# A kernel of linear attention and two expert layers: transposing q as loaded, wider weight blocks, and a new order of the front

## The chip, the cores and the metric

One core of a Trainium2 chip runs the whole program. The metric is the device time of one execution in microseconds, from runs of the same program on the chip; the profile is of one execution of it. TensorE (PE) makes all matrix products and transposes, VectorE (DVE) and ScalarE (ACT) copy, add, split and square, GpSimd (POOL) clears tiles and takes the inverse roots, and SyncE (SP) issues nearly all transfers.

## What is computed

```python
kv = np.einsum('bhsd,bhse->bhde', k, v)          # 4 batches, 8 heads, 576 tokens, 64 wide
out = np.einsum('bhsd,bhde->bhse', q, kv)
out = out / np.sqrt(np.mean(out * out, -1) + 1e-06) * g_norm
x = out as [2304, 512]                            # heads side by side
x = ((x @ w1) * (x @ w2) @ w3) @ w_out            # float64 weights, d_ff 1024
p = domain_probs / domain_probs.sum(-1)           # 4 experts
out = sum over e of p[:, e] * (max(x @ e_w1[e], 0) @ e_w2[e])
```

## The kernel before

Every large product is split: an operand is kept as a high and a low part of a rounded 32-bit type (fp32r), and a product is three matmuls (`mm3`, L327 to L329), high by high, high by low and low by high. Many products are joined in a scheme of seven block products in place of eight, which needs sums of blocks of the weights (s1 to s4) and of the tokens (t1 to t4). The attention's own products are plain float32.

The order of the work on every engine is made ahead by a planner (`Plan`). Each step is added with the engines that could run it and a cost on each, what it reads and writes, and its delay (`latency`); `order` then runs through the steps with these costs and writes down one fixed sequence for each engine. The steps come in stages: the text `FRONT` lists those up to the experts, and the stage's number is the priority. Costs and delays are only the planner's; on the chip an engine waits for what its next instruction needs.

The front of the kernel. `constants` makes an identity and ten warm-up transposes of it (L424). A `unit b p` is one batch and two heads: it loads q, k and v as [128 partitions, 2 heads x 4 tokens x 64], which is 512 tokens with four to a partition; the remaining 64 tokens of all heads come through `rest_kv` as one tile of 64 partitions for each of k and v and a batch, with cleared partitions below (L571). Then

- `outer` (L717) makes kv of the two heads, each from 4 rounds of 128 tokens and one of the rest; head 0 goes to partitions 0 to 63 and columns 0 to 63 of a bank, head 1 to partitions 64 to 127 and columns 64 to 127. Two copies bring them to the diagonal blocks of `kvb`, a cleared tile for a batch (L670).
- `qs` is a copy of q with its columns in the order token, head (L733 on ScalarE, L734 on VectorE), so that a transpose (L688) gives both heads of one token round in one block; `inner` (L745) multiplies four such blocks by the diagonal block of `kvb`.
- `normed_turned` sums the squares (L596: eight ScalarE instructions with a running sum each), takes the inverse root on POOL (L608, L609), scales (L612), transposes (L688), multiplies by g and splits.

`rest_unit` does the inner products of the 64 remaining tokens of two batches (L780). g comes in as a column, one element for each partition (`load_norm`, issued by ScalarE). In stages 1, 2 and 3 the planner's loop puts 3, 3 and 2 transposes of the identity (L1822, "fillers") before a step that opens a new bank.

`weight n f` loads and decodes 128 columns and all 512 rows of w1 or w2 (float64, 512 KB). `bilinear_plain` and `bilinear_pair` multiply x by two of these each and multiply the results. After `mixed` and `mixed_product`, the experts run over three groups of 768 tokens: `up` makes the hidden layer of one pair of F blocks, `down` or `down_product` multiplies by the second layer. In the first group the expert's weights are loaded (`expert_weights`, two transfers for each layer and pair of blocks, i and i + 4), summed, split and stored to DRAM (`keep_w2`, L1317, one buffer for an expert); later steps load them back (`right_operand`, as `w`).

Of the kernel before, what the change touches and what calls it, by code (L numbers as in the profile page):

```python
# [31 lines left out]
SUMMING = 18  # L32
# [67 lines left out]
class Plan:  # L100
# [11 lines left out]
    def add(self, engines, emit, reads=(), writes=(), latency=0.2, stage=None, free=False, hold=None):  # L112
# [4 lines left out]

        op = Op(engines, emit, self.stage if stage is None else stage, latency)
# [24 lines left out]
    def order(self):  # L143
# [43 lines left out]
        while len(result) < len(ops):  # L187
# [9 lines left out]
            for e in engines:  # L197
# [26 lines left out]
                end = now + op.engines[e]  # L224
# [5 lines left out]
                op.done = end + op.latency  # L230
# [32 lines left out]
def attention_moe_kernel(  # L263
# [48 lines left out]
    plan = Plan({"r": RAWS, "h": TILES, "n": 4, "c": 2, "b": BANKS, "d": 1000, **RINGS})  # L312
# [33 lines left out]
    def load(buf, *parts, key=None, queue="sp", cost=None):  # L346
        def emit(_):
            for dst, src in parts:
                (nc.sync if queue == "sp" else nc.scalar).dma_start(
                    out=dst(buf.tile), in_=src[:, :] if isinstance(src, Buf) else src  # L350
                )

        add(
            {queue: cost or (1.48 if buf.kind == "r" else 0.68)}, emit,
            reads=[src for _, src in parts if isinstance(src, Buf)], writes=[(buf, key)], latency=2.6,
        )
# [54 lines left out]
    graw = const.tile([P, 1], F32, name="graw")  # L411
# [5 lines left out]
    def constants():  # L417
# [3 lines left out]
        nc.scalar.activation(out=graw, in_=ident[:, 0:1], func=ACTF.Square)  # L421
# [4 lines left out]
    def load_norm(_):  # L426
        for i in range(2):
            nc.scalar.dma_start(out=graw[i * D:(i + 1) * D], in_=g_norm.rearrange("(d o) -> d o", o=1))
        nc.vector.tensor_scalar(out=g8, in0=graw, scalar1=float(D) ** 0.5, scalar2=None, op0=ALU.mult)
# [19 lines left out]
    def decode(name, src, shape=None):  # L449
# [6 lines left out]
        load(raw, ((lambda t: t.rearrange("p (k f) -> p k f", k=KD)) if shape else whole, src))  # L456
# [110 lines left out]
    def rest_kv(b):  # L567

        kvr[b] = [half("kvr") for _ in (k, v)]
        for raw, src in zip(kvr[b], (k, v)):  # L570
            add({"pool": 0.4}, lambda _, raw=raw: nc.gpsimd.memset(raw[REM:P], 0.0), writes=[(raw, 1)])  # L571
            load(
                raw, (lambda t: t[0:REM].rearrange("p (h d) -> p h d", d=D), rest(src, b)),
                key=0, cost=1.05,
            )
# [3 lines left out]
    def normed_turned(ps, places, whole_values=None):  # L579
# [7 lines left out]
        summing = SUMMING > len(summed)  # L587
# [23 lines left out]
        def scale(e):  # L611
            nc.vector.tensor_tensor(  # L612
# [5 lines left out]
        if summing:  # L618
            add({"act": 8 * t_act(D, True)}, square, reads=[ps], writes=[t, ss])
# [3 lines left out]
        add({"pool": 1.91}, root, writes=[ss], hold=0.3)  # L623
# [44 lines left out]
    def zeroed(name):  # L668
        t = half(name)
        add({"pool": 0.5}, lambda _: nc.gpsimd.memset(t.tile, 0.0), writes=[t])  # L670
        return t
# [21 lines left out]
    def unit(b, p):  # L693
        first = b not in kvb
        if first:
            kvb[b] = zeroed("kvb")
        loaded = []
        for name, src in (("q", q), ("kv", k), ("kv", v)):
            raw = half(name, ring="attention")
            load(raw, (heads, head_pair(src, b, p)), cost=0.82)  # L700
            loaded.append(raw)
        qraw, ks, vs = loaded
        if first:
            rest_kv(b)
        kr, vr = kvr[b]
        ps = bank()

        def outer(e):
            for r in range(R + 1):
                for h in range(2):  # L710
                    c = slice(h * D, (h + 1) * D)
                    if r < R:
                        a, b_ = heads(ks.tile)[:, h, r, :], heads(vs.tile)[:, h, r, :]
                    else:
                        m = slice(p * P + h * D, p * P + (h + 1) * D)
                        a, b_ = kr[:, m], vr[:, m]
                    nc.tensor.matmul(ps[c, c], a, b_, start=r == 0, stop=r == R)  # L717

        add({"pe": 0.9}, outer, reads=[ks, vs, kr, vr], writes=[ps])
        for i in range(2):  # L720
            c = slice(i * D, (i + 1) * D)
            evacuate(
                kvb[b], ps, D, lambda t, i=i, c=c: t[c, p * P + i * D:p * P + (i + 1) * D],
                lambda t, c=c: t[c, c], key=(p, i),
            )
        qs = half("qs")

        def by_token(t):
            return t.rearrange("p (r h d) -> p h r d", r=R, h=2)

        add(
            {"act": t_act(512), "dve": t_fast(512)},
            lambda e: nc.scalar.copy(by_token(qs.tile), heads(qraw.tile)) if e == "act"  # L733
            else nc.vector.tensor_copy(out=by_token(qs.tile), in_=heads(qraw.tile)),  # L734
            reads=[qraw], writes=[qs],
        )
        pq = turned(qs)
# [9 lines left out]
        add({"pe": 0.86}, inner, reads=[qt, (kvb[b], (p, 0)), (kvb[b], (p, 1))], writes=[po])  # L747
        xr[b, p] = half("xr")
        if b == B - 1 and p < HP // 2:
            normed_turned(po, [], xr[b, p])  # L750
        else:
            xt[b, p] = Pair("xt")
            normed_turned(po, [(512, xt[b, p], whole, whole, None)], xr[b, p])

    def rest_unit(g):
# [4 lines left out]
            (lambda t: t[REM:P].rearrange("p (h d) -> p h d", d=D), rest(q, 2 * g + 1)), cost=1.5,  # L760
# [21 lines left out]
        add({"pe": 1.72}, inner, reads=[qs[0], qs[1], kvb[2 * g], kvb[2 * g + 1]], writes=[po])  # L782
# [16 lines left out]
    def first_product(w, xs, b):  # L799
# [3 lines left out]
        for k0 in range(0, KD, 2):  # L803
# [4 lines left out]
            def mms(_, k0=k0):  # L808
# [1046 lines left out]
```

## Time and profile before

| | us |
|---|---|
| median of 3 runs (1107.46 to 1109.48) | 1107.79 |
| the profiled execution | 1109.42 |
| its span, first to last instruction | 1107.6 |
| TensorE busy in the span | 1093.7 |
| VectorE / ScalarE / GpSimd busy | 864.2 / 616.5 / 47.0 |
| granted TensorE clock | full (2.4 GHz) in all slices |

Busy time is the union of an engine's instructions; matmuls are pipelined and their ends are modelled, so instructions that follow each other overlap, and the chain of waits, which lays them end to end, shows better what one of them costs.

### The profile page before, as it was taken

The numbers are of one execution on the slowest core, as the hardware profiler recorded it, in microseconds if no ns is written. First come the engines' busy times: TensorE is split into PE (matmuls) and PEld (weight loads), VectorE is DVE, ScalarE is ACT, GpSimd is POOL, SyncE is SP. The second block draws the span as 40 slices with busy tenths as digits, with TensorE's granted clock in tenths as the row PEclk, the third lists the DMA queues.
The fourth block names the chain that finished last, engine by engine and source line by source line (L and its number), as shares of the span: only waits on it lengthen the run. The fifth ranks groups of instructions, "written<-read, shape, count | busy, mean of one in ns | idle before, by whom it ended". The sixth has DMA issues, their size and how long they took to land.

```text
span 1107.6 us, 18599 instructions
## 1 busy us (share of the span) xinstructions
PE 1093.7 (99%) x6376; PEld 993.9 (90%) x6376; DVE 864.2 (78%) x1723; ACT 616.5 (56%) x1500; POOL 47.0 (4%) x57
## 2 busy tenths in 40 slices
PE   7999999999999999999999999999999999999998
PEld 6888888888888999999998999999999999999998
DVE  4888888889869887878888884557788866485896
ACT  6998754656636665754564465443455555444531
POOL 4513200000000000000000000000000000000000
PEclk9999999999999999999999999999999999999999
DMA  9999993441230499988999996878779877686856
GB/s 262 292 345 331 379 359 124 135 155 37 88 103 17 156 334 352 355 304 285 353 356 355 369 348 222 284 237 283 239 240 356 298 222 257 226 290 219 278 154 196
DMA packets 176862, 282.30 MB, mean 255 GB/s; under 512 B 22144, under 2 KB 89728, under 8 KB 176768
## 3 DMA queue, kind: packets, MB, share of 16 engines
q1 hardware_dynamic: 176448, 280.85, 76.1%
q8 instruction: 50, 0.82, 0.3%
q10 hardware_dynamic: 320, 0.26, 0.1%
q14 instruction: 44, 0.36, 0.1%
HBM read 198.22 MB, written 82.84 MB: 254 GB/s over the span
## 4 chain that ended last, share of the span: by engine, by line
PE 94%; DMA 3%; ACT 1%; POOL 1%; DVE 0%; issue 0%; SPq 0%; POOLq 0%; DVEq 0%
PE b L327 24%; PE b L329 24%; PE b L328 24%; PE b L1574 18%; PE b L688 2%; DMA kv<-in_v_dram 1%; PE b L745 1%; PE b L717 1%; DMA w<-w2kept 1%; DMA graw<-in_g_norm_dram 0%; POOL ss L609 0%; DMA we<-wel 0%; DMA woraw<-in_moe_w_out_dram 0%; PE b L780 0%; ACT x L596 0%
## 5 line engine op out<-in xcount | busy, mean ns | idle before, releaser
L676 ACT COPY u<-b 128x384 f32<-128x384 f32 (+1 forms) x191 | 96.4, 505 | 209.3 <-PE b L329 202.3
L1574 PE MATMUL b<-w,hth 128*128 128x512 f32 x588 | 208.2, 394 | 0.3 <-DVE acc L1602 0.2
L1410 DVE TENSOR_TENSOR u<-u,b 128x384 f32<-128x384 f32 x144 | 79.5, 552 | 117.9 <-PE b L329 59.3
L1574 PE MATMUL b<-w,htl 128*128 128x256 f32 x588 | 153.9, 279 | 0.0
L1574 PEld LDWEIGHTS b<-w,hth 128*128 128x128 f32 x588 | 108.4, 188 | 19.0 <-DVE acc L1602 0.9
L1574 PEld LDWEIGHTS b<-w,htl 128*128 128x128 f32 x588 | 110.6, 188 | 3.8
L1602 DVE SCALAR_TENSOR_TENSOR acc<-b,pn,acc 128x512 f32<-128x512 f32 x123 | 85.5, 745 | 29.1 <-PE b L1574 28.4
L372 ACT CAST hth<-s 128x384 fp32r<-128x384 f32 x144 | 70.0, 512 | 48.3 <-DVE s L1510 45.6
L1421 ACT ACTIVATE u<-u 128x384 f32<-128x384 f32 x108 | 56.9, 527 | 44.0 <-DVE u L1410 43.7
L377 DVE TENSOR_TENSOR htl<-s,hth 128x384 fp32r<-128x384 f32 x144 | 75.4, 551 | 3.4 <-ACT hth L372 3.1
L329 PE MATMUL b<-wdh,htl 128*128 128x512 f32 x144 | 56.7, 394 | 0.0
L377 DVE TENSOR_TENSOR htl<-u,hth 128x384 fp32r<-128x384 f32 x108 | 56.0, 551 | 0.8 <-ACT hth L372 0.7
L328 PE MATMUL b<-wdl,hth 128*128 128x512 f32 x144 | 56.6, 393 | 0.0
L327 PE MATMUL b<-wdh,hth 128*128 128x512 f32 x144 | 56.0, 389 | 0.0
L372 ACT CAST hth<-u 128x384 fp32r<-128x384 f32 x107 | 51.5, 510 | 2.4 <-PE b L329 2.0
L327 PE MATMUL b<-w,hth 128*128 128x256 f32 x168 | 47.6, 284 | 1.3 <-DMA w<-w2kept 1.3
L328 PE MATMUL b<-w,hth 128*128 128x256 f32 x168 | 47.5, 283 | 0.0
L329 PE MATMUL b<-w,htl 128*128 128x256 f32 x168 | 47.5, 283 | 0.0
L327 PE MATMUL b<-th,weh 128*128 128x512 f32 x112 | 44.6, 398 | 0.2 <-ACT u L676 0.2
L329 PE MATMUL b<-th,wel 128*128 128x512 f32 x112 | 43.7, 390 | 0.0
L328 PE MATMUL b<-tl,weh 128*128 128x512 f32 x112 | 43.7, 390 | 0.0
L956 DVE TENSOR_TENSOR u<-u,b 128x512 f32<-128x512 f32 x42 | 28.7, 686 | 16.0 <-PE b L329 9.2
(297 smaller groups left out, 3165.5 us busy)
## 6 DMA issues: line engine op xcount, KB each, us to landing
w<-w2kept SPq DMA_DIRECT2D x126, 512.0 KB, 4.4
we<-we SPq DMA_DIRECT2D x240, 256.0 KB, 5.3
we<-weh SPq DMA_DIRECT2D x48, 256.0 KB, 4.4
we<-wel SPq DMA_DIRECT2D x48, 256.0 KB, 4.2
e2raw<-in_moe_w_dram SPq DMA_DIRECT2D x40, 256.0 KB, 4.5
w3raw<-in_moe_w_dram SPq DMA_DIRECT2D x16, 512.0 KB, 3.8
e1raw<-in_moe_w_dram SPq DMA_DIRECT2D x32, 256.0 KB, 4.6
w2kept<-wth SPq DMA_DIRECT2D x32, 256.0 KB, 4.4
```

The source lines that it names most:

```text
L327: nc.tensor.matmul(ps, w[0], x[0], start=first, stop=False, skip_group_check=more)
L328: nc.tensor.matmul(ps, w[0], x[1], start=False, stop=False, skip_group_check=more)
L329: nc.tensor.matmul(ps, w[1], x[0], start=False, stop=last, skip_group_check=more)
L372: nc.scalar.copy(to(dst.high.tile), value(src.tile))
L377: nc.vector.tensor_tensor(out=to(dst.low.tile), in0=value(src.tile), in1=to(dst.high.tile), op=ALU.subtract)
L676: lambda e: nc.scalar.copy(to(dst.tile), value(src.tile)) if e == "act"
L688: nc.tensor.transpose(ps[:, c], raw[:, c], ident)
L956: lambda _: nc.vector.tensor_tensor(out=t.tile, in0=t.tile, in1=ps.tile, op=ALU.add),
L1410: lambda _: nc.vector.tensor_tensor(out=t[:, :W], in0=base[:, :W], in1=ps[:, :W], op=ALU.add),
L1421: lambda eng: nc.scalar.activation(out=t[:, :W], in_=src[:, :W], func=ACTF.Relu)
L1574: nc.tensor.matmul(ps.tile if whole_width else ps[:, 0:256], (h.high if whole_width else h.low)[:, c], both if whole_width else raw[:, r, ...
L1602: nc.vector.scalar_tensor_tensor(out=a.tile, in0=ps.tile, scalar=sc, in1=a.tile, op0=ALU.mult, op1=ALU.add)
```

## The change

- **q as loaded.** The copy `qs` goes; the transpose takes q's own tile, so that a block holds one head and two tokens of a partition. `inner` needs the same head's kv on both diagonal blocks; `outer` writes both heads to partitions 0 to 63 and two copies put them on both halves. There are two `kvb` tiles for a batch in place of one. The scaling step writes the columns back in the order token, head.
- **Rest of k and v.** Two tokens a partition on 32 partitions, four heads a tile: 16 loads of 64 KB in place of 8 of 128 KB, and two rounds in `outer` in place of one.
- **w1, w2.** A weight tile is 256 rows by 256 columns; a pair of F blocks is 2i and 2i + 1 in place of i and i + 4. The block sums are taken by views.
- **g.** Two loads of a row of 64, a transpose on TensorE, and a scaling on VectorE.
- **Experts.** F blocks side by side in one transfer for each layer; fewer, wider sums, some of them in place in the loaded tile; the order of operands s2, s1 and t2, t3, t1 with a sign turned in both factors of one product; the kept second layer in a buffer for each group of operands and half of the F blocks.
- **Planner.** Delays of 0.04 in place of 0.2 behind other engines than TensorE, a margin for ScalarE, VectorE and SP, SP's costs by 1.02, some costs changed; six of the 18 sums of squares (`EARLY`) by one ScalarE pass and a VectorE reduction.
- **The list** `FRONT` is new.

```diff
-SUMMING = 18
+TRAFFIC = 1.02
+MARGIN = {"act": 0.1, "dve": 0.1, "sp": 0.2}
+EARLY = (3, 4, 5, 8, 14, 15)
 FILL = {1: 3, 2: 3, 3: 2}
-    "norm_scale, weight 0 7, unit 1 3, unit 1 2, weight 1 4, weight 1 0, unit 1 0, unit 1 1, unit 0 0, "
-    "unit 0 2, unit 0 1, unit 0 3, unit 2 0, bilinear_plain 0 0, weight 0 3, unit 3 1, bilinear_pair 0 3, "
+    "norm_scale, unit 1 2, unit 1 3, weight 1 4, unit 1 1, weight 1 0, unit 1 0, unit 0 1, unit 0 2, unit "
+    "0 0, unit 3 1, unit 0 3, weight 0 3, unit 3 0, bilinear_plain 0 0, unit 2 1, bilinear_pair 0 3, unit "
...
-    graw = const.tile([P, 1], F32, name="graw")
+    graw = const.tile([1, P], F32, name="graw")
...
-            nc.scalar.dma_start(out=graw[i * D:(i + 1) * D], in_=g_norm.rearrange("(d o) -> d o", o=1))
+            nc.scalar.dma_start(out=graw[:, i * D:(i + 1) * D], in_=g_norm.rearrange("(o d) -> o d", o=1))
...
-            add({"pool": 0.4}, lambda _, raw=raw: nc.gpsimd.memset(raw[REM:P], 0.0), writes=[(raw, 1)])
+    def rest_kv(b, j):
+        turn = sum(at[1] == j for at in kvr) % 2
+        if (turn, j) not in kvr_slots:
+            kvr_slots[turn, j] = [half("kvr") for _ in (k, v)]
+            for raw in kvr_slots[turn, j]:
+                for at in ((REM // 2, REM), (REM, P)):
+                    cleared(raw, at)
...
+                    lambda t: t[0:REM // 2].rearrange("p (h r d) -> p h r d", h=HP, r=2),
+                    src[b, j * HP:(j + 1) * HP, M:S, :].rearrange("h (p r) d -> p h r d", r=2),
...
         def outer(e):
-            for r in range(R + 1):
+            for r in range(R + 2):
                 for h in range(2):
-                    c = slice(h * D, (h + 1) * D)
...
-                    nc.tensor.matmul(ps[c, c], a, b_, start=r == 0, stop=r == R)
+                    nc.tensor.matmul(
+                        ps[0:D, h * D:(h + 1) * D], a, b_, start=r == 0 and h == 0, stop=r == R + 1,
+                        skip_group_check=True,
+                    )
...
-        pq = turned(qs)
+        pq = turned(qraw)
...
-            for r in range(R):
-                c = slice(r * P, (r + 1) * P)
-                nc.tensor.matmul(po[:, c], qt[:, c], kvb[b][:, p * P:(p + 1) * P], start=True, stop=True)
+            for j in range(4):
+                c, m = slice(j * P, (j + 1) * P), at + j // 2 * P
+                nc.tensor.matmul(po[:, c], qt[:, c], own[:, m:m + P], start=True, stop=True)
...
-            for h in range(HP):
-                c = slice(h * P, (h + 1) * P)
+            for h in range(H):
+                c = slice(h // 2 * P, (h // 2 + 1) * P)
                 for i in range(2):
-                    nc.tensor.matmul(po[:, c], qs[i][:, c], kvb[2 * g + i][:, c], start=i == 0, stop=i == 1)
+                    own, at = kvb[2 * g + i][h // 4], h % 4 * P + h % 2 * D
+                    nc.tensor.matmul(
+                        po[:, h * D:(h + 1) * D], qs[i][:, c], own[:, at:at + D], start=i == 0, stop=i == 1
+                    )
...
-            weights[n, f] = decode(f"w{n + 1}", columns((moe_w1, moe_w2)[n], f), True)
+            half_, i = divmod(f, KF // 2)
+            src = (moe_w1, moe_w2)[n][half_ * 256:(half_ + 1) * 256, i * 256:(i + 1) * 256]
+            weights[n, f] = decode(f"w{n + 1}", src.rearrange("(k p) f -> p k f", p=P), 2)
...
-        load(raw1, *(
-            (lambda t, n=n: t[:, n].rearrange("p (k f) -> p k f", k=KD), columns(e_w1[e], f))
-            for n, f in enumerate(fs)
-        ))
-        load(raw2, *((lambda t, n=n: t[:, n], e_w2[e][f * P:(f + 1) * P, :]) for n, f in enumerate(fs)))
-        w, _ = winograd_weights([raw1, raw1], [lambda t: t[:, 0], lambda t: t[:, 1]])
+        load(raw1, (whole, e_w1[e][:, i * 256:(i + 1) * 256].rearrange("(k p) f -> p k f", p=P)))
+        load(raw2, (whole, e_w2[e][i * 256:(i + 1) * 256, :].rearrange("(n p) c -> p n c", p=P)))
+        w = expert_operands(raw1)
...
-        if e not in w2_kept:
-            w2_kept[e] = Buf("d", f"w2kept{e}", [P, len(W2_OPERANDS), KF // 2, 2, 256], F32, tag=f"w2kept{e}")
+        for k in range(*which):
+            if (e, k, i // 2) not in w2_kept:
+                name = f"w2kept{e}_{which[0]}_{i // 2}"
+                w2_kept[e, k, i // 2] = (
+                    w2_kept[e, which[0], i // 2][0] if k > which[0]
+                    else Buf("d", name, [P, n, 2, 2, 256], F32, tag=name), k - which[0],
+                )
...
+        ps = bank()
+        add(
+            {"pe": 0.1}, lambda _: nc.tensor.transpose(ps[:, 0:1], graw, ident[0:1, 0:1]),
+            reads=[row_], writes=[ps],
+        )
```

`expert_operands`, which is new, makes the same operands as `winograd_weights` did by three sums (256, 512 and 256 columns wide) in place of four of 256, the first and third in place in `raw1`; `w2_sums` does likewise in the second layer's tile; `block_weights` makes those of w1 and w2 by views of two tiles.

## Rows read from the trace of the kernel before

**Rows 1.** The head of the page: span; busy time, share, instructions.
```profile
span 1107.6 us, 18599 instructions
...
PE 1093.7 (99%) x6376; PEld 993.9 (90%) x6376; DVE 864.2 (78%) x1723; ACT 616.5 (56%) x1500; POOL 47.0 (4%) x57
```

**Rows 2.** Busy us by stretch: PE, PEld, DVE, ACT, POOL; clock, DMA share, GB/s.
```profile
0.00:10.00 10.00, 7.10 (x52) 6.80 (x52) 1.61 (x4) 3.80 (x6) 6.71 (x19) 1.00 0.88 213
10.00:20.00 10.00, 6.98 (x71) 5.97 (x73) 5.82 (x11) 7.74 (x43) 2.77 (x3) 1.00 1.01 321
...
30.00:40.00 10.00, 9.48 (x111) 8.15 (x111) 8.23 (x16) 9.94 (x60) 6.64 (x7) 1.00 1.13 270
...
45.00:130.00 85.00, 85.00 (x574) 72.00 (x573) 74.17 (x139) 74.19 (x268) 19.64 (x20) 1.00 1.03 343
```

**Rows 3.** Who TensorE waited for: us in total, times, longest.
```profile
PE b L717 <- DMA kv<-in_v_dram: 3.6, 3, 1.7
...
PE b L327 <- DMA w<-w2kept: 1.3, 1, 1.3
```

**Rows 4.** The chain that ended last, its longest pieces: start, us, what.
```profile
43.88 0.24 PE b L328
...
46.42 0.89 PE b L745 x8
...
50.51 0.73 PE b L717 x20
...
61.42 1.32 PE b L717 x40
...
103.70 1.79 PE b L780 x16
...
480.67 5.94 DMA w<-w2kept
```

**Rows 5.** TensorE's instructions in order of time, from the start: start, us, what.
```profile
1.34 4.64 PE L424 MATMUL warm<-ident 128*128 128x128 f32 x20 [1.34 <-POOL ident masks.py:199]
5.77 0.88 PE L1822 MATMUL b<-ident 128*128 128x128 f32 x6
...
9.04 0.69 PE L717 MATMUL b<-kv 128*64 128x64 f32 x16 [1.28 <-DMA kv<-in_v_dram]
...
10.63 0.34 PE L717 MATMUL b<-kvr 128*64 128x64 f32 x4 [0.90 <-DMA kvr<-in_v_dram]
```

**Rows 6.** TensorE's groups, 0 to 45 us: busy us, mean ns, idle before.
```profile
L745 PE MATMUL b<-kvb,qt 128*128 128x128 f32 x64 | 8.8, 281 | 0.5 <-ACT kvb L676 0.3 <-DVE kvb L677 0.2
L717 PE MATMUL b<-kv 128*64 128x64 f32 x144 | 6.2, 227 | 3.7 <-DMA kv<-in_v_dram 3.6
L1822 PE MATMUL b<-ident 128*128 128x128 f32 x40 | 6.1, 284 | 0.0
L688 PE MATMUL b<-ident,qs 128*128 128x128 f32 x36 | 5.7, 280 | 0.9 <-ACT qs L733 0.7
...
L688 PE MATMUL b<-ident,x 128*128 128x128 f32 x28 | 4.3, 276 | 0.0
...
L327 PE MATMUL b<-xth,wh 128*128 128x512 f32 x7 | 3.0, 427 | 0.0
```

**Rows 7.** The same view in three narrow windows, at 50.47, 50.56 and 50.64 us.
```profile
50.44 0.28 PE L717 MATMUL b<-kv 128*64 128x64 f32 x2
...
50.44 0.34 PE L717 MATMUL b<-kv 128*64 128x64 f32 x4
...
50.44 0.39 PE L717 MATMUL b<-kv 128*64 128x64 f32 x6
```

**Rows 8.** Who SP's queue waited for, 0 to 45 us.
```profile
SPq L349 <- DMA graw<-in_g_norm_dram: 2.4, 1, 2.4
```

**Rows 9.** POOL's instructions in order of time, from the start.
```profile
1.28 0.52 POOL L670 MEMSET kvb<- 128x512 f32 x1
1.86 0.98 POOL L571 MEMSET kvr<- 64x512 f32 x2
```

More of the change, by code (lines that the diff above doesn't have):

```diff
@@ L669, in zeroed @@
         t = half(name)
-        add({"pool": 0.5}, lambda _: nc.gpsimd.memset(t.tile, 0.0), writes=[t])
+        cleared(t, (0, P))
         return t
@@ L699, in unit @@
             raw = half(name, ring="attention")
-            load(raw, (heads, head_pair(src, b, p)), cost=0.82)
+            load(raw, (heads, head_pair(src, b, p)), cost=0.8)
             loaded.append(raw)
         qraw, ks, vs = loaded
-        if first:
-            rest_kv(b)
-        kr, vr = kvr[b]
+        if (b, p // 2) not in kvr:
+            rest_kv(b, p // 2)
+        kr, vr = kvr[b, p // 2]
         ps = bank()
         def outer(e):
-            for r in range(R + 1):
+            for r in range(R + 2):
                 for h in range(2):
-                    c = slice(h * D, (h + 1) * D)
                     if r < R:
@@ L905, in pair_weights @@
                 ]
-                for m, pair in enumerate(dict.fromkeys(pair for pair, _ in made[0].values()))
+                for m, pair in enumerate(dict.fromkeys(pair for pair, *_ in made[0].values()))
             ]
@@ L1317, in keep_w2 @@
             lambda _: nc.sync.dma_start(
-                out=kept.tile[:, which[0]:which[1], i, part, :],
+                out=kept.tile[:, :, i % 2, part, :],
                 in_=t.tile.bitcast(F32)[:, 0:256 * n].rearrange("p (o c) -> p o c", o=n),
             ),
-            reads=[t], writes=[(kept, (which, i, part))], latency=2.4,
+            reads=[t], writes=[(kept, (i, part))], latency=2.4,
         )
@@ L1330, in w2_sums @@
             raw = Buf("r", "e2raw", [P, 2, 512], F32)
-            load(raw, *(
-                (lambda t, n=n: t[:, n], e_w2[e][f * P:(f + 1) * P, :]) for n, f in enumerate((i, i + KF // 2))
-            ))
-        def part(n, c):
-            return lambda: [raw[:, n, c * 256:(c + 1) * 256]]
-        def own(t, c):
-            return lambda: [t[:, c * 256:(c + 1) * 256]]
-        t12, t34 = half("t12"), half("t34")
-        lo, hi = slice(0, 256), slice(256, 512)
-        combined("t1", 256, part(0, 1), part(0, 0), ALU.subtract, [raw], t12, lo)
@@ L1344, in w2_sums @@
-        combined("t2", 256, part(1, 1), own(t12, 0), ALU.subtract, [raw, (t12, 0)], t12, hi)
-        combined("t3", 256, part(1, 1), part(0, 1), ALU.subtract, [raw], t34, lo)
-        combined("-t4", 256, part(1, 0), own(t12, 1), ALU.subtract, [raw, (t12, 256)], t34, hi)
-        for t, which in ((t12, (3, 5)), (t34, (5, 7))):
-            s = Pair("wt")
-            split(s, t, 512)
+            load(raw, (whole, e_w2[e][i * 256:(i + 1) * 256, :].rearrange("(n p) c -> p n c", p=P)))
+        t23 = half("t23")
@@ new lines, in sums @@
+        def sums(make, reads, writes, n):
+            add({"dve": t_dve(n)}, make, reads=reads, writes=writes)
+        sums(
+            lambda _: nc.vector.tensor_tensor(
+                out=raw[:, 0, 0:256], in0=raw[:, 0, 256:512], in1=raw[:, 0, 0:256], op=ALU.subtract
+            ), [], [raw], 256,
+        )
+        sums(
+            lambda _: nc.vector.tensor_tensor(
+                out=t23[:, :].rearrange("p (o c) -> p o c", o=2),
+                in0=raw[:, 1, 256:512].unsqueeze(1).to_broadcast([P, 2, 256]),
+                in1=raw[:, 0].rearrange("p (o c) -> p o c", o=2), op=ALU.subtract,
+            ), [raw], [t23], 512,
+        )
@@ new lines, in w2_sums, with two @@
+        sums(
+            lambda _: nc.vector.tensor_tensor(
+                out=raw[:, 1, 0:256], in0=raw[:, 1, 0:256], in1=t23[:, 0:256], op=ALU.subtract
+            ), [t23], [raw], 256,
+        )
+        t14 = Pair("wt")
+        def two(t):
+            return t.rearrange("p (o c) -> p o c", o=2)
+        add(
+            {"act": t_act(512), "dve": t_fast(512)},
+            lambda eng: nc.scalar.copy(two(t14.high.tile), raw[:, :, 0:256]) if eng == "act"
+            else nc.vector.tensor_copy(out=two(t14.high.tile), in_=raw[:, :, 0:256]),
+            reads=[raw], writes=[t14.high],
+        )
@@ L1350, in w2_sums @@
+        add(
+            {"dve": t_dve(512)},
+            lambda _: nc.vector.tensor_tensor(
+                out=two(t14.low.tile), in0=raw[:, :, 0:256], in1=two(t14.high.tile), op=ALU.subtract
+            ),
+            reads=[raw, t14.high], writes=[t14.low],
+        )
+        t23s = Pair("wt")
+        split(t23s, t23, 512)
+        for s, which in ((t14, (5, 7)), (t23s, (3, 5))):
             for n, p in enumerate(s.parts):
```

244 lines of the change are left out of this document (173 added, 71 removed), and 20 rows, old and new, of the table FRONT.

## The prediction

> **What bounds the kernel now.** I read the head of the profile first: TensorE is busy for 1093.7 of 1107.6 us [rows 1], so at most 13.9 us can come from making it wait less, and whatever is added to its own work is added to the time wherever it has no wait to put it into. Then the busy time by stretch [rows 2]: the missing time lies almost wholly in the first 40 us (2.90 and 3.02 us in the first two stretches of 10 us, 0.52 in the fourth), while from 45 to 130 us TensorE is busy for all of 85 us, although units of the attention still run there. VectorE and ScalarE are near 74 of 85 us in that stretch, so they are close behind but not ahead. Then who waited for whom [rows 3]: TensorE's named waits are the k and v loads of the first units (3.6 us in three waits) and later one wait of 1.3 us for the kept second-layer weights, which the chain of waits shows as a transfer of 5.94 us from 480.67 us [rows 4].
>
> Busy flatters the front, though: ten warm-up transposes run from 1.34 us on, with the fillers behind them [rows 5], and 40 filler instructions (L1822) stand among the first units' work [rows 6]. What counts is the useful work done by 45 us, where waiting ends. The price of one instruction comes from the chain, which takes them back to back [rows 4]: 0.89 us for 8 with 128 float32 columns is 0.111 us each; a unit's 20 outer instructions take 0.73 us; one 512-column product of the split type takes 0.24 us. By 45 us there are [rows 6] 64 of L745 (7.1 us), 144 of L717 on k and v, 16 a unit, so nine units (6.6), 36 + 28 transposes at the same 0.111 (7.1), and 19 products in three lines, L327's 7 standing for them (4.5): 25.3 us. So 19.7 us went elsewhere: 1.34 until the identity exists, 4.4 of warm-up until the first filler at 5.77 [rows 5], 40 x 0.111 = 4.4 filler, and 9.5 of waiting.
>
> **The change part by part.** *The outer products* decide. Before, head 0 of a pair writes partitions 0 to 63 of its bank and head 1 partitions 64 to 127. The narrow windows [rows 7] show what this does: instructions come in twos, 2, then 4, then 6 of them ending at 0.28, 0.34 and 0.39 us, so two are done in 0.055 to 0.06 us. Two units in a row take 1.32 us for 40 [rows 4], or 0.033 each, which is well under half of the 0.111 of a product twice as wide: the two heads run side by side. After the change both heads write partitions 0 to 63, so the halves of the array can no longer be shared out, and each instruction needs a step of its own: 0.059 us, which is the step from one product to the next in the same half (1.32 less 0.73 us for ten more twos), or at least half of 0.111 = 0.0556. There are also 24 instead of 20, because the 64 remaining tokens come as two tokens on 32 partitions. A unit goes from 10 twos to 24 singles: 14 x 0.059 = 0.826 us more, 16 units 13.2 us. Bounds: if two still overlapped, 2 x 0.059 x 16 = 1.9; at 0.0556, 16 x (24 x 0.0556 - 0.59) = 11.9; at the price of the 128-column product, 16 x (24 x 0.111 - 0.59) = 33, which I leave out of the range since the same half already takes a new product with its own weights every 0.059. I take 13.2.
>
> The Trainium skill, page "TensorE: Matmul & The Clock Gate", section "Why this matters for your kernels", speaks against this edit: products with few output rows should each be placed at their own strip of PSUM partitions, so that they run concurrently, and the change gives that up. Rows 7 agree with it. That page's Part 3 puts the cost of a second tile beside the first at about 4 ns; by that a single would take 0.059 - 0.004 and the sixteen units would cost 16 x (24 x 0.055 - 0.59) = 11.7 us (an estimate with that page's figure) in place of 13.2.
>
> *The rest units' inner products* become 16 of 64 columns in place of 8 of 128, that is 32 instructions where 16 took 1.79 us [rows 4]. At 0.059 that is 1.89, or +0.1 each, +0.2 for two. Between the ends 0 (0.0556) and +3.5 (as slow as 128 columns: 32 x 0.111 less 1.79, twice) I take the low one, because the outer products of the same width are the nearest row. The transpose of g is one product more, 0.1.
>
> *The front.* The first outer ran at 9.04 us and then stopped for the rest of k and v until 10.63 [rows 5]; ahead of it stood a 512 KB weight load, two 128 KB loads of runs of 256 B, and the 128 single elements of g, on whose transfer SP's queue sat for 2.4 us [rows 8]. The new list starts with a unit, its rest loads are 64 KB, and g is two rows. So the first loads should land about when the warm-up ends. The fillers of stages 1 and 2 now stand in two units, three for each of four banks: 24 transposes, 48 instructions, 5.3 us. After that a unit asks TensorE for about 0.73 + 0.83 + two times 0.44 + 0.89 = 3.3 us, while its three 256 KB loads take 2.4 us at the 321 GB/s of the second stretch [rows 2]. TensorE, not the loads, then sets the pace. What can't go away is 1.34 + 4.4 + 5.3 = 11.0 us; I allow 1.1 of waiting for the norm chain of the first units, so 12.1 in place of 19.7: a gain of 7.6. Ends: 8.7 with no wait, and 3 if the waits only move. This includes the removed copy `qs`, whose wait was 0.7 us [rows 6].
>
> *The kept weights.* One buffer for each group of operands and half of the F blocks lets the load at 480.67 us go before the last store: the 1.3 us wait goes. What is late next is the second half, whose blocks are needed some 12 products later. Ends 0 and -1.5.
>
> *At nothing:* the qs copies, the six sums of squares made by one ScalarE pass and a reduction on VectorE, the three-instruction sums of the expert weights, the wider runs of w1, w2 and the expert blocks, all lie beside a TensorE that is busy all the time from 45 us [rows 2]; if that cover failed, they would be gains, not costs. They leave the number of large products unchanged. POOL clears more: twelve more k, v pieces and four more kvb tiles, at 0.49 to 0.52 us [rows 9] some 6 us of more memsets than before, 12.2 in all. The first norm needs POOL only after an inner product, a square and the fillers, past 14 us, so the queue is clear by then; on SP's queue 16 rest loads stand in place of 8. The new transposition of g waits for its load on TensorE's queue; behind it stand the first unit's transposes, which have the fillers as cover.
>
> Sum: 13.2 + 0.2 + 0.1 - 7.6 - 1.3 = +4.6 us. The profiled execution has a span of 1107.6 and took 1109.42 us, 1.6 above the median of 1107.79; that execution would become 1114.0, the median **1112.4**.
>
> **Rivals.** *A: as worked out*, slower, alone from 1108.5 to 1117. Chance 0.56.
> *B, the other side: the heads still share the array.* Mechanism: a 64-column product leaves the array's second half or its input free enough that the next one starts early, although it writes the same partitions. For it: the engine takes two weight loads and two products within 0.059 us already. Against it: in rows 7 each half moves on only once in 0.055 to 0.06, and half of 0.111 is the time that its columns need. Then 1.9 replaces 13.2 and the time is 1101.1, faster. It decides from a price of 0.041 us for one instruction: 16 x (24 x 0.041 - 0.59) = 6.3, and 6.3 + 0.3 - 7.6 - 1.3 = -2.3. Chance 0.15.
> *C: the front gives all it can.* No wait at all (8.7), singles at 0.0556 (11.9), 1.5 for the kept weights, nothing on the rest units: 11.9 + 0.1 - 8.7 - 1.5 = +1.8, so 1109.6, no difference. For it: with dearer outers TensorE lags behind the plan and its gaps close. Chance 0.18.
> *D: the list does less than it should.* The named waits move to the norm chain and the decoding, ScalarE being busy 9.94 of 10 us from 30 to 40 us [rows 2]; the front gives 3, and the narrow products of the rest units cost 1.8 each: 13.2 + 3.5 + 0.1 - 3 - 1.3 = +12.5, or 1120.3 at the worst; with one of the two alone it is 1117.0 (front at 3) or 1115.7 (narrow products). Chance 0.11.
>
> **How the numbers follow.** Something of 0.2% (2.2 us) is about what a measurement of this kernel can tell from no change. Faster by more: B with 0.15, and 0.02 from the edge of C. Within: the bulk of C and a low edge of A (a front gain a little over mine), 0.25. Slower by more: the rest of A, and D: 0.58. The range 1103 to 1117 leaves out most of B and the worst of D, some 0.18.
>
> **What would show it.** Right: one unit's 24 outer instructions take 1.4 us or more back to back, single starts about 0.059 us apart; the first outer starts between 6 and 8 us; TensorE has no named DMA wait of over 1 us after it; the wait at 480 us is gone. Wrong: outers in twos again, ScalarE or VectorE named before TensorE's idle time between 15 and 60 us, or waits on raw buffers in the expert stages, where the in-place sums hold a load's tile longer.

## The result, and the profile after

The changed kernel took 1121.08 us in the median of four executions (1120.77 to 1121.79), the kernel before 1108.55 beside it: a ratio of 1.0114, 95% interval [1.0097, 1.0132]. It is slower, as forecast, but by 12.5 us where 4.6 were forecast, and it lies above the range, which ended at 1117. The profiled execution took 1121.27 us with a span of 1119.5, 11.9 more than the span before.

The head of the page of the changed kernel, and its busy time in two stretches (columns as in rows 2):

```profile
span 1119.5 us, 18619 instructions
...
PE 1110.4 (99%) x6481; PEld 1011.5 (90%) x6481; DVE 863.8 (77%) x1690; ACT 605.8 (54%) x1401; POOL 52.9 (5%) x69
```
```profile
0.00:45.00 45.00, 43.25 (x434) 40.05 (x434) 21.91 (x40) 29.70 (x127) 28.82 (x46) 1.00 0.97 289
45.00:130.00 85.00, 83.87 (x586) 72.83 (x585) 65.73 (x124) 64.80 (x221) 24.05 (x23) 1.00 0.84 266
```

TensorE now waits less than before (9.1 us not busy against 13.9 in rows 1) and yet ends 12 us later: what it does itself has grown. Its busy time is 16.7 us longer, and the two kinds of products priced below make 13.0 and 3.5 of that. ScalarE is busy 10.7 us less in all (605.8 for 616.5), VectorE 0.4 less; from 45 to 130 us, where they were near 74 us each [rows 2], they now have 66 and 65, and nothing came of it.

Who TensorE waited for, all of it (rows 3 are those of before):

```profile
PE b L331 <- ACT u L702: 2.2, 4, 0.9
...
PE b L331 <- DMA w<-w2kept: 0.5, 1, 0.5
PE b L766 <- ACT kvb L752: 0.2, 1, 0.2
```

No wait for q, k or v is left. The wait for the kept weights is 0.5 in place of 1.3. New are four waits, 2.2 us, at 97, 127, 192 and 537 us, for copies on ScalarE.

The chain that ended last: a unit's outer products, the rest units' inner products, the kept weights (rows 4 have 0.73 for L717, 1.79 for L780, 5.94):

```profile
8.11 1.54 PE b L742 x24
...
107.01 3.52 PE b L802 x32
...
491.02 6.69 DMA w<-w2kept
```

The outer products one by one, at the ends of three narrow windows (8.07, 8.16, 8.24 us; rows 7 are those of before), and the rest units' products in the same manner with their weight loads (PEld):

```profile
8.04 0.27 PE L742 MATMUL b<-kv 128*64 128x64 f32 x1
...
8.04 0.33 PE L742 MATMUL b<-kv 128*64 128x64 f32 x2
...
8.04 0.39 PE L742 MATMUL b<-kv 128*64 128x64 f32 x3
```
```profile
106.74 0.30 PEld L802 LDWEIGHTS b<-kvb,qr 128*128 128x128 f32 x2
...
106.85 0.22 PE L802 MATMUL b<-kvb,qr 128*128 128x64 f32 x1
...
106.85 0.33 PE L802 MATMUL b<-kvb,qr 128*128 128x64 f32 x2
...
106.85 0.45 PE L802 MATMUL b<-kvb,qr 128*128 128x64 f32 x3
```

In the first, one product is added where rows 7 have two, at the same step of about 0.06 us. In the second, each product of 64 columns adds 0.11 us, as much as one of 128 columns in rows 4 (0.89 for 8).

TensorE's work from 0 to 45 us (rows 6 are those of before):

```profile
L742 PE MATMUL b<-kv 128*64 128x64 f32 x151 | 10.9, 225 | 0.0
L766 PE MATMUL b<-kvb,qt 128*128 128x128 f32 x72 | 9.7, 279 | 0.4 <-ACT kvb L752 0.2
L1987 PE MATMUL b<-ident 128*128 128x128 f32 x48 | 7.0, 283 | 0.0
L714 PE MATMUL b<-ident,q 128*128 128x128 f32 x36 | 5.7, 282 | 0.0
L742 PE MATMUL b<-kvr 128*64 128x64 f32 x72 | 5.7, 222 | 0.0
...
L714 PE MATMUL b<-ident,x 128*128 128x128 f32 x28 | 4.2, 272 | 0.0
L331 PE MATMUL b<-xth,wh 128*128 128x512 f32 x2 | 0.9, 448 | 0.0
```

By the prediction's own count: 72 inner products (8.0 us), 151 + 72 outer instructions or 9.3 units at 1.54 (14.3), 64 transposes (7.1) and 6 large products (1.4) are 30.9 us of useful work in 45, so 14.1 us went elsewhere, in place of 19.7. Yet only 6 large products are done by then where 19 were: the front does more useful work, and the outers eat it.

### The profile page after: what moved, and what is told of

Read it like the earlier page. It is cut to its first block, busy times and chain, and to the rows that moved or that the text cites. A ratio compares the mean times of both kernels' runs of the same rounds, so it can differ in the third digit from the quotient of the medians.

```text
span 1119.5 us, 18619 instructions
## 1 busy us (share of the span) xinstructions
PE 1110.4 (99%) x6481; PEld 1011.5 (90%) x6481; DVE 863.8 (77%) x1690; ACT 605.8 (54%) x1401; POOL 52.9 (5%) x69
## 4 chain that ended last, share of the span: by engine, by line
PE 95%; DMA 2%; ACT 1%; DVE 1%; issue 0%; SPq 0%; POOL 0%; POOLq 0%; ACTq 0%
PE b L331 24%; PE b L333 24%; PE b L332 24%; PE b L1725 18%; PE b L742 2%; PE b L714 2%; PE b L766 1%; PE b L802 1%; DMA w<-w2kept 1%; PE b L1987 1%; DMA w3raw<-in_moe_w_dram 1%; DMA e2raw<-in_moe_w_dram 0%; PE warm L428 0%; ACT u L702 0%; DMA ab0kept<-u 0%; DMA we<-weh 0%
## 5 line engine op out<-in xcount | busy, mean ns | idle before, releaser
L1725 PEld LDWEIGHTS b<-w,hth 128*128 128x128 f32 x588 | 108.5, 188 | 19.7 <-DVE acc L1753 0.9
L1661 DVE TENSOR_TENSOR s<-u 128x384 f32<-128x384 f32 x72 | 37.6, 552 | 2.9 <-ACT u L1572 2.9
```

The lines of the kernel that those rows point to most:

```text
L1661: lambda eng: nc.vector.tensor_tensor(out=t[:, :W], in0=x[:, :W], in1=y[:, :W], op=op),
L1725: nc.tensor.matmul(ps.tile if whole_width else ps[:, 0:256], (h.high if whole_width else h.low)[:, c], both if whole_width else raw[:, r, ...
```

## The experiments

The theory after the result: TensorE is bound by its own instructions; the outer products cost 13.0 us, the rest units 3.5, the fillers stand on its path, and the front's gain is real but smaller. The rival: the new list and the waits it makes cost most of it. Times are medians; the kernel before took 1109.5, 1108.9, 1109.1 and 1109.2 us beside the four groups of runs.

**Heads apart again.** In the changed kernel the outer products go back to two halves (and four copies in place of two):

```diff
-                    nc.tensor.matmul(
-                        ps[0:D, h * D:(h + 1) * D], a, b_, start=r == 0 and h == 0, stop=r == R + 1,
-                        skip_group_check=True,
-                    )
+                    c = slice(h * D, (h + 1) * D)
+                    nc.tensor.matmul(ps[c, c], a, b_, start=r == 0, stop=r == R + 1)
...
```

> The changed kernel with one edit: head 0 of a pair writes partitions 0 to 63 of the bank and head 1 partitions 64 to 127 again, still with two rounds of the rest tokens; four copies of 64 columns in place of two of 128 bring them to the kvb blocks. Theory (TensorE's own work): in the trace of the changed kernel a unit's 24 outer instructions come one by one every 0.0585 us and take 1.42 us. As twelve twos they take 0.75, so 16 units give back 16 x 0.7 = 11 us; some 1 to 3 us of waiting for the first units' loads comes back, since a unit then asks TensorE for 2.6 us and its loads take 2.4. So 1110 to 1113. Rival (the new list and its waits cost most of the 12 us): the outers hide in the front as the loads come no sooner, and only the seven units after 40 us count, 5 us, and the copies add waits: 1116 to 1121.

Measured: 1116.2 us, 1.0060 [1.0040, 1.0079] of before, 4.9 less than the changed kernel. A unit's outer products in its chain, its waits, and its busy time by stretch:

```profile
91.47 0.85 PE b L743 x24
```
```profile
PE b L331 <- ACT u L702: 4.9, 3, 3.3
PE b L714 <- DMA q<-in_q_dram: 1.6, 4, 0.9
...
PE b L743 <- DMA kv<-in_v_dram: 1.2, 1, 1.2
```
```profile
180.00:186.00 6.00, 6.00 (x28) 4.99 (x27) 5.02 (x10) 2.13 (x4) 0.00 (x0) 1.00 1.00 294
186.00:190.00 4.00, 0.70 (x4) 0.24 (x2) 0.00 (x0) 1.15 (x3) 0.00 (x0) 0.88 0.89 323
190.00:196.00 6.00, 5.96 (x14) 4.70 (x15) 3.53 (x6) 3.78 (x7) 0.00 (x0) 0.51 0.98 356
196.00:200.00 4.00, 4.00 (x19) 3.25 (x18) 4.00 (x9) 1.16 (x2) 0.00 (x0) 1.00 0.09 32
```

The price is as the theory has it: 1.54 to 0.85 is 0.69 a unit, 11 us in all. But the time lies outside the theory's 1110 to 1113, at the lower edge of the rival's 1116 to 1121, and part of what the rival said came true: waits for loads came back in the front (TensorE is busy for 39.9 of the first 45 us, in place of 43.3), and at 186 us it waits 3.3 us for a copy that stands on ScalarE behind the decoding of a late w3 load. After that wait the granted clock is 0.51 for 6 us, nearly all of it at the 1.2 GHz level, and 14 products are done where 28 were in the 6 us ahead. So a wait of 3.3 us cost some 6. That execution took 1119.7 us, 3.5 above the median of its kernel, so it is one of the worse cases.

**The rest units' products in one of 128 columns**, the two heads' columns read with a gap:

```diff
-            for h in range(H):
+            for h in range(HP):
...
+                    both = own[:, at:at + 2 * P].rearrange("p (x d) -> p x d", d=D)[:, 0:4:3, :]
```

> The changed kernel with one edit: the rest units' inner products take both heads of a block in one product of 128 columns, read from two blocks of kvb with a gap between, so 16 instructions in place of 32 for a unit. The planner's order is the same. Theory: each of the 32 instructions pays for its own load of 128 weight columns (0.11 us, the step in the trace of the changed kernel), so half of them give back half of 3.52 us, twice: 1.75 x 2 = 3.5, so 1117.6. Rival: the price lies in the streaming of columns or in reading the cleared blocks; then the same 64 + 64 columns cost the same and the time stays 1121.

Measured: 1117.8 us, 1.0075 [1.0055, 1.0095]; 3.3 less than the changed kernel, where 3.5 was forecast.

**The same products with 64 weight columns**, each batch in its own half:

```diff
+                    c = slice(h // 2 * P + i * REM, h // 2 * P + (i + 1) * REM)
...
+                        po[i * REM:(i + 1) * REM, h * D:(h + 1) * D], qs[i][:, c], own[:, at:at + D],
```

> The changed kernel with one edit: the rest units' inner products keep 64 columns and 32 instructions for a unit, but each loads only the 64 weight columns of its own batch and writes only that batch's 64 partitions, so that two batches stand in the two halves of the array. Theory: weight loads set the price of a narrow product; with 64 weight columns in two halves two instructions take 0.0585 us, a unit's 32 take 0.95 in place of 3.52, two units give back 5.1 us: 1116.0. If the halves took turns: 32 x 0.0585 = 1.87, 3.3 back, 1117.8. Rival (a product of this line costs 0.11 whatever it loads): 1121.

Measured: 1116.9 us, 1.0063 [1.0044, 1.0082]; 4.2 less, where 5.1 was forecast. The first of two rest units in the chain, of the kernel with wide products and of that with halves:

```profile
107.79 1.79 PE b L803 x16
```
```profile
107.26 1.08 PE b L802 x32
```

The second decides: the same 32 instructions over the same 64 moving columns take 1.08 us in place of 3.52 when the weights are 64 columns wide and two stand side by side. Side by side alone could at most halve 3.52, to 1.76; the rest came with the narrower weights. And in the first, an instruction over 128 moving columns costs what one over 64 did (1.79 for 16, 3.52 for 32). So the price of these products went by the columns of their weights, not by their moving columns. Whether the weight load itself makes it, or the wider output, these runs don't separate.

**No fillers** (`FILL = {}`) in the changed kernel.

> The changed kernel without the 24 filler transposes (48 instructions) in the first two units. Theory: with the early loads and dear outers TensorE is never short of work from 6 us on, so the fillers (5.9 us by their steps) stand on its path and most of them come back: 4 to 5.9 us less, 1115 to 1117. Rival 1: they stand where TensorE would wait for the norms, copies and loads of the first units anyway: 0 to 1.5 us less. Rival 2: without them the granted clock falls in the first 20 us and the time grows.

Measured: 1117.6 us, 1.0068 [1.0051, 1.0085]; 3.5 less, a little under the forecast of 4 to 5.9. In the profiled execution, which took 1115.9, TensorE is busy for 41.4 of the first 45 us in place of 43.3: 1.9 of the 5.9 us went into waits that opened in the front, loads first:

```profile
PE b L742 <- DMA kv<-in_v_dram: 1.2, 2, 0.8
...
PE b L714 <- DMA q<-in_q_dram: 0.4, 1, 0.4
```

**The kernel before with both heads in one half**, the price alone, with 20 instructions:

```diff
...
-                    nc.tensor.matmul(ps[c, c], a, b_, start=r == 0, stop=r == R)
+                    nc.tensor.matmul(
+                        ps[low, c], a, b_, start=r == 0 and h == 0, stop=r == R, skip_group_check=True
+                    )
...
```

> The kernel before with one edit: both heads' outer products go to partitions 0 to 63, one after the other (still 20 instructions). Theory: 20 single steps of 0.0585 in place of ten, 0.585 us more a unit, 9.4 us of TensorE's work in 16 units; the front of the kernel before waits 7.6 us for loads and copies, and some 4 to 5 of the nine early units' 5.3 us go into these waits, while the seven later units add 4.1 in full: 4.5 to 6 us more than before. Rival (no wait absorbs anything, since the loads are bound to the work): 9.4 more. Rival (it costs nothing, heads share the array anyway): 0 to 1 more.

Measured: 1114.7 us beside 1108.9, 1.0047 [1.0030, 1.0064], 5.8 more. A unit in its chain, and its waits for k and v (3.6 in rows 3):

```profile
27.14 1.31 PE b L718 x20
...
63.19 2.48 PE b L718 x40
```
```profile
PE b L718 <- DMA kv<-in_v_dram: 1.3, 2, 1.0
```

Twenty more singles take 2.48 - 1.31 = 1.17 us, 0.0585 each. 1.31 - 0.73 = 0.58 a unit is 9.3 us, of which about 3.5 went into waits that were there anyway. This is the theory's number, and it shows what the front of the kernel before could absorb: no more than that.

**The list of the kernel before** in the changed kernel.

> The changed kernel with the list of the kernel before. Theory: the new list gives the early first unit (no weight load ahead of it) and takes 1.5 us in later waits; with dear outers the front is bound by TensorE under either list, so the old one costs the 1.6 us of the first weight load and gives back up to 1.5: 1119 to 1123. Rival (the list makes the late waits and is the larger part of the loss): 1116 or less. Rival (the list makes the whole front gain of 6.7 us): 1125 or more.

Measured: 1121.3 us, 1.0110 [1.0095, 1.0125], no difference from the changed kernel. The new list neither costs nor brings anything here; both rivals fall.

**g as a column again** in the changed kernel.

> The changed kernel with g loaded as a column again, 128 single elements, without the transpose. Theory: in the front of the changed kernel TensorE is bound by its own work, so a transfer of some 5 us that delays other loads is hidden but for the first unit: 0 to 1.5 us more, 1121 to 1123. Rival (g as a row is what brings the first outer from 9.0 to 8.0 us and ends the stall of the rest loads): 2 to 4 us more.

Measured: 1121.0 us, 1.0107 [1.0083, 1.0130], no difference from the changed kernel; the rival falls.

**What is left of the change without the two dear products.** Outer and rest products on halves, first with the new list and no fillers, then with the old list and fillers, then with the old list and none:

> The changed kernel with the heads' outer products on two halves, the rest units' inner products on two halves with 64 weight columns each, and no fillers. Theory: 11 us of outer products, 5 of rest products and 3 to 4 of fillers come back, less 4 to 7 us of waits that open in the front and behind late loads of w3: 1106 to 1110, at or a little under the kernel before. Rival (once TensorE is quicker every wait that its work hid appears, and the loads bound the front): 1112 or more.

> The changed kernel with outer and rest products on two halves and the list of the kernel before, fillers kept. Theory: 16 us of TensorE's work come back and the waits are those of a list that was set to outers of this price: 1106 to 1110. Rival (the late waits come from the planner's shorter delays, not from the list): 1112 or more, with ScalarE's copies named as in the run with the heads apart.

> The changed kernel with outer and rest products on two halves, the list of the kernel before and no fillers. With the fillers it took 1110.2. Theory: without them the front waits 2 to 3 us more for copies and norms and gives the rest of their 5.3 us back: 1107 to 1108. Rival (the loads bound the front once the outers are cheap): 1110, no change. If the granted clock falls behind a longer wait in the front: 1111 or more.

Measured: 1110.8 (1.0014 [1.0002, 1.0025]), 1110.2 (1.0006 [0.9995, 1.0016]) and 1108.6 (0.9996 [0.9986, 1.0007]). The three medians are within 0.2% of the kernel before, and each is 0.2 to 0.8 us above the end of its forecast. The second differs from the run with the old list in these two edits alone: 1121.3 and 1110.2, so the two kinds of products make 11.1 us, nearly the whole loss. Waits of the first and the third, and the third's busy time in two stretches of the front:

```profile
PE b L714 <- DVE x L633: 3.0, 6, 1.2
PE b L331 <- ACT u L702: 2.3, 3, 1.7
PE b L714 <- DMA q<-in_q_dram: 2.1, 2, 1.8
```
```profile
PE b L743 <- DMA kv<-in_v_dram: 2.9, 4, 1.4
PE b L765 <- ACT qt L702: 1.8, 2, 1.5
```
```profile
6.00:10.00 4.00, 2.56 (x31) 2.24 (x32) 2.57 (x5) 1.58 (x4) 3.73 (x8) 0.81 1.09 297
10.00:14.00 4.00, 2.96 (x35) 2.70 (x33) 0.69 (x1) 3.36 (x22) 1.94 (x4) 0.77 1.04 362
```

So the rest of the change (q as loaded, the smaller rest loads, g, the wider blocks, the buffers) moves the time by nothing that can be told: with cheap outers TensorE waits for loads and norms in the front again. In the third, TensorE being busy for 2.6 and 3.0 of 4 us, the granted clock is 0.81 and 0.77, so the lower of its two levels for a part of each stretch. The first has no fillers either, and its front keeps 1.00.

**The kernel before with its rest units on halves**, and the same without fillers and with its first weight load behind two units:

```diff
-                    nc.tensor.matmul(po[:, c], qs[i][:, c], kvb[2 * g + i][:, c], start=i == 0, stop=i == 1)
+                    m = slice(h * P + i * REM, h * P + (i + 1) * REM)
+                    nc.tensor.matmul(
+                        po[i * REM:(i + 1) * REM, c], qs[i][:, m], kvb[2 * g + i][:, c], start=True, stop=True
+                    )
```

> The kernel before with one edit: the rest units' inner products load only the 64 weight columns of their own batch and write its 64 partitions, 128 columns wide, so that two batches stand in two halves of the array. Theory: 16 instructions in twos of 0.11 take 0.9 us in place of 1.79, twice, while TensorE is busy throughout: 1.7 to 1.8 us less than before, 0.16%. Rival (two products of 128 columns don't run side by side, or later waits take the gain): 0.

> The kernel before with the rest units' products on two halves, no fillers, and its first weight load listed behind the first two units. Theory: 1.8 us from the rest units; the first units' data come some 1.5 us sooner; the fillers stand mostly in waits there, so 1 to 2 of their 4.4 us come back: 3 to 5 us less than before. Rival (the loads bound this front to their own pace, whichever comes first, and a wait takes the place of each filler): 1.5 to 2.5 less. Rival (the weight that comes later is missed at the first large product): no gain.

Measured: 1107.5 (0.9987 [0.9976, 0.9998]) and 1108.4 (0.9991 [0.9982, 1.0000]). The first has the lowest median of this study, 1.5 us under the kernel before, where 1.7 to 1.8 was forecast; its rest unit takes 1.02 us for 16 in place of 1.79. The second gained nothing more, where 3 to 5 us was forecast. In its front the clock fell, as the stretch from 18 to 22 us shows, after one in which TensorE was busy for 1.77 of 4 us. Its mean granted clock is 0.994 to 0.997 in all twelve executions, and 0.996 to 1.000 in the twelve of the first. How much of the missing gain that makes isn't shown.

```profile
104.73 1.02 PE b L781 x16
```
```profile
14.00:18.00 4.00, 1.77 (x27) 1.37 (x27) 3.35 (x8) 3.98 (x22) 2.56 (x3) 1.00 1.09 348
18.00:22.00 4.00, 2.53 (x36) 2.31 (x32) 3.38 (x8) 3.05 (x9) 1.57 (x1) 0.54 1.15 310
```

**The late waits.** At 537 us ScalarE's cast waits for the second expert layer's load, which is now one transfer of 512 KB, and TensorE's copy stands behind the cast:

```profile
536.75 0.62 ACT L376 CAST wdh<-e2raw 128x512 fp32r<-128x512 f32 x1 [1.33 <-DMA e2raw<-in_moe_w_dram]
537.28 0.47 ACT L702 COPY u<-b 128x384 f32<-128x384 f32 x1
```

Two transfers put back into the changed kernel, and one put into the kernel before:

> The changed kernel with the second expert layer's tile loaded by two transfers of 256 KB (one for each block of 128 rows) in place of one of 512 KB, as the kernel before has it. Theory: the wait of 1.0 us at 536 us in the changed kernel comes from this: ScalarE's cast of the first block waits 1.33 us for the whole transfer and TensorE's copy stands behind it; with two transfers the first block lands some 0.7 us sooner and the wait at that place shrinks by about that: 0.5 to 1.2 us less in all. Rival (the transfer is late because of the queue ahead of it, not of its size): no difference.

> The kernel before with the second expert layer's pair of blocks loaded by one transfer of 512 KB in place of two of 256 KB. Theory (size of the transfer): a wait of about 1 us behind ScalarE's cast appears near 530 us and the time grows by 0.5 to 1.2 us. Rival (the queue ahead of it): no difference.

Measured: 1121.3 us, 1.0122 [1.0107, 1.0137], and 1109.1, 1.0002 [0.9988, 1.0017]: no difference in either, and both theories miss. In the first the wait at 537 us is gone, but its waits behind ScalarE's copies still sum to 2.4 us, as the others have grown:

```profile
PE b L331 <- ACT u L702: 2.4, 3, 1.2
```

In the kernel before with one transfer no wait of 1 us appears: from 500 to 560 us its waits behind such copies are 0.2 us. So the size of that transfer made that wait at most in the changed kernel, and it doesn't set the time. What makes such waits come back elsewhere isn't settled.

## Why the prediction was right or wrong, point by point

| term | forecast | measured | from |
|---|---|---|---|
| outer products | +13.2 | 16 x (1.54 - 0.73) = +13.0 | chain, rows 4 |
| rest units | +0.2 | 2 x (3.52 - 1.79) = +3.5 | chain, rows 4 |
| transpose of g | +0.1 | +0.1 | |
| front | -7.6 | 14.1 - 19.7 = -5.6 | counts above, rows 6 |
| kept weights | -1.3 | 0.5 - 1.3 = -0.8 (not shown to be the change's) | waits, rows 3 |
| copies on ScalarE, late | 0 | 2.2 - 0.2 = +2.0 | waits |
| sum | +4.6 | +12.2, the spans differ by 11.9 | |

**The outer products** were right to 0.2 us, and the run with one half in the kernel before shows the same price alone. Rival B (the heads still share the array) is refuted by the single steps.

**The rest units** were the largest miss. The step that failed is the choice between two bounds: "I take the low one, because the outer products of the same width are the nearest row". They have the same moving width but half the weight columns. The far end, +3.5, was the measured value: each product takes 0.11 us in place of 0.059. The runs give four prices for one float32 instruction: 0.111 with 128 weight and 128 moving columns, 0.11 with 128 and 64, 0.0585 with 64 and 64, and about 0.12 for two with 64 and 128 side by side (1.02 for 16). The wider of the two sets it in all four. The nearest row was L745, with the same 128 weight columns. None of the signs of being wrong looked at the rest units.

The Trainium skill, "TensorE: Matmul & The Clock Gate", Part 3, says in its list of what overlaps that a weight load overlaps a product in flight only when the row groups differ (its paragraph on the mechanism also allows it through a background weight buffer). The rows here disagree with the list: the record of L802's loads runs for 0.30 us from 106.74, across the start of its products at 106.85, over the same 128 rows. And load and product don't add up: halving the moving columns to 64 took nothing off the 0.11 us.

**The front** gave 5.6 of 7.6, and two steps of it failed. The first is the reading of 9.5 us as waiting. In the kernel before, TensorE was idle for only 6.2 us of the first 45 after the identity existed; the other 3.3 lay inside its busy time.

```profile
0.00:45.00 45.00, 37.51 (x387) 33.22 (x388) 27.52 (x53) 34.58 (x175) 23.59 (x35) 1.00 1.03 269
```

The forced part was right (warm-up, fillers, the start: 11 us). I allowed 1.1 us of waiting; 3.1 remained, of which 0.4 is idle time and 2.7 again lies inside the busy time. The chain of the changed kernel shows a part of that as dearer steps between groups of unlike products: a unit's 24 steps of 0.0585 are 1.40 and it has 1.54, and six fillers take 0.86 us behind outer products and 0.67 behind transposes. That this makes all of the 2.7 is argued, not shown.

```profile
9.65 0.86 PE b L1987 x6
...
10.96 0.67 PE b L1987 x6
```

The second step is the cause. I put the gain down to first loads that land sooner, through the list, the row of g and the smaller rest loads; the runs with the old list and with g as a column lost nothing, so neither of these two brought it. And the gain and the dear outers are partly the same time. One half in the kernel before, with nothing else changed, raises TensorE's busy time in the first 45 us from 37.5 to 41.2; with the heads apart the changed kernel's falls from 43.3 to 39.9, and under the old list, with the rest products on halves too, from 43.45 to 41.42. So some 2 to 4 us of the waits that went were filled by the outers' own work, and that the sum of the two terms came near is luck in part. What took away the rest (smaller rest loads, the dropped copy, the planner's delays) was not run alone. What I wrote of the pace was right beside dear outers: no load was waited for, and TensorE set it.

**At nothing** held as far as the runs can tell: with both kinds of products on halves, all the rest of the change moved the time by nothing clear. (The clearing was miscounted: eight more k, v pieces, not twelve; POOL's busy time grew by the 6 us that were forecast.) But the heading had no place for waits that appear anew, and four did, 2.0 us. Where they come from was followed for one of them, and removing it moved the time nowhere. Their sum differs between executions: 0.5 to 4.9 us in the profiled ones of the other runs of the changed kernel, 0.2 to 1.5 in those of the kernel before.

**The kept weights**: the 0.8 us isn't shown to be the change's. The wait is 0 to 0.8 us in the other runs of the changed kernel and 0 to 0.9 in those of the kernel before, so it differs as much without the change. The awaited load leaves at 491.0 us, where it left at 480.7 before; that it went earlier, as I forecast, isn't seen.

**The signs.** A unit's 24 outers took 1.54 us, one by one; the first started at 8.04 us, just past the 6 to 8 that I gave; no load was waited for longer than 0.5 us; the wait for the kept weights shrank but stayed.

**The range** ended below the result although rival D had the sum: both the rest units' far end and a front of 3, 1120.3, left out of the range as its worst case at a chance of 0.11. That it comes within 0.8 us of the result is half luck: its narrow products came at their price, but the front gave 5.6, and the late waits, which it didn't have, took 2.0. From the forecast the way is 1112.4 + 3.3 + 2.0 + 2.0 + 0.5 = 1120.2.

## What to carry to other kernels

On an engine that is busy 99% of the time, count its instructions first: an edit that spares another engine 11 us and takes away 5 us of waits is worth nothing if it makes narrow products take turns. Before merging outputs onto the same partitions, look whether the instructions were starting in twos. A cost that fills waits and a gain from waits that go are one term, not two. And price a narrow float32 product by the wider of its weights and its columns, taking a row with the same weights.

## What the runs showed of the hardware that was not expected

A float32 product of 64 columns with 128 weight columns takes 0.11 us, as long as one of 128 columns; with 64 weight columns in two halves two take about 0.067 us (1.08 for 32). And the granted clock (1.00 is 2.4 GHz, the lower level is 1.2 GHz) falls behind waits, in one execution and not in another: 0.51 for 6 us after 3.3 us without work, at 186 us in the run with the heads apart; 0.54 to 0.81 in the front of two kernels without fillers, where TensorE was waiting for 1.0 to 2.2 of 4 us in the same stretch or the one ahead of it; and with fillers too, in the kernel before with its rest units on halves, where no single wait was longer than 1.8 us:

```profile
10.00:14.00 4.00, 2.02 (x13) 1.79 (x14) 3.02 (x6) 1.45 (x4) 0.00 (x0) 0.68 1.08 346
14.00:18.00 4.00, 4.00 (x21) 3.77 (x21) 2.05 (x5) 1.49 (x10) 0.00 (x0) 0.50 1.10 349
```

Against it, the first of the three kernels with both products on halves was busy for 1.67 of 4 us from 10 to 14 us, without fillers, and stayed at 1.00. Of the 69 executions of the kernel before beside these runs, 21 have a mean clock of 1.000 and a median of 1108.0 us, and 14 have 0.997 or less and a median of 1110.3: part of that kernel's scatter goes with its clock, while the changed kernel's four lie at 0.999 to 1.000 and within 1.0 us.

Taking out 5.9 us of fillers gave back 3.5 us in the changed kernel, and in the kernel with cheap outers and the old list 1.6 (1110.2 to 1108.6), which is not clear of noise.
